# A two-layer spectral mixer on one core: batch 0's spectra made twice for one filter tile

## The chip, the cores and the metric

The kernel runs on one core of a Trainium2 chip. Its time is the device time of one launch in microseconds (us). The core has a matrix engine (TensorE, PE in the profile), three engines for elementwise work (VectorE or DVE, ScalarE or ACT, GpSimd or POOL) and a queue engine (SyncE or SP). Each takes its own instructions in order and waits for the others by semaphores. Data move by DMA, issued from the queues of SP, ACT and POOL.

## The reference

```python
def _attn_ref(x, filt_r, filt_i):            # x: (8, 3136, 256)
    X = np.fft.rfft(x, axis=1)
    F = (filt_r + 1j * filt_i)[None, :, :]   # (1569, 256)
    return np.fft.irfft(X * F, n=x.shape[1], axis=1)

def _moe_ref(x, U, V, w_ch1, w_ch2):         # x is the result above
    h = x.transpose(0, 2, 1) @ U @ V         # rank 32 along the sequence
    u = x + h.transpose(0, 2, 1)
    return u + np.maximum(u @ w_ch1, 0.0) @ w_ch2   # 256 -> 1024 -> 256
```

## The kernel before, in words

The transform of length 3136 = 64 x 49 is done in two steps by matrix products. Step one is a transform over 64 rows (table `w64`). Step two is, for each of 32 residues s, a product with the table `t2[s]` (98 x 128), whose 128 outputs are 64 real and 64 imaginary parts of one group of frequencies. The spectrum is multiplied by the filter, which lies in the tile `ft`, and goes back by the table `g12` (128 x 98 for each s). The residues go in pairs: m = 0 to 15 stands for s = 2m and 2m + 1. The tables and the filter come in four parts (`PARTS`) of 8 residues, so a new part begins at m = 0, 4, 8 and 12.

Batch 0 is a prologue of its own. All of it is in this order:

- `load_x`, `load_rest`, `load_table`, `load_filters` issue the loads from POOL's queue: batch 0 of x in three chunks, the tables and the filter part by part, then batch 1 of x, then U, V and the two channel weights.
- `first_f1` does step one in twelve units of four matmuls each, and the odd last row at its end. ACT and DVE empty PSUM into `at`, two instructions a unit, one on each. `keep_on(n)` puts n matmuls without use into the PE queue, and `keep_in` does so on another tile.
- `first_a(m)` turns a pair into place (four matmuls) and ACT copies it to `a`.
- `first_mid` is a pipeline over m: `forward` makes the spectrum px (two matmuls), `both_products` multiplies it on DVE by two filter sections at once into `uv` (1024 columns), `back` (eight matmuls with the two sections of `g12`) makes pi, and ACT copies pi into `et` with two instructions. px is made two pairs ahead, `a` three pairs ahead.
- Then `et` is transposed into `e2`, while `f1_units(1, True)`, drawn with `next(fill)`, does step one of batch 1. Its 13 units are drawn at set places.

In the old filter layout the section 0 of `ft` holds the real filter on both halves of the 128 partitions and section 1 holds the imaginary one, minus on the second half. The loads fill partitions 0 to 48 alone. `swap_real` and `swap_imag` on DVE make the second halves, a part at a time, before the first pair that needs the part. The second section of `g12` is the first with its halves exchanged: part 0 is loaded ready (`gs`), the others are made by `swap_table` on POOL.

After the prologue comes the stream: groups of rows run through `mm1` (256 to 1024), a ReLU, and `mm2` (1024 to 256). All the other work of the later batches is put by hand into slots between these products (`put(slot, generator)`); a group of eight slots takes some 9 us. Batch 1's middle (`both_products` again) starts in slot 8.8 at 1.2 slots a pair, batch 2 uses `product`, which multiplies in three instructions on DVE.

Of the kernel before, what the change touches and what calls it, by code (L numbers as in the profile page):

```python
# [13 lines left out]
SEQ = 3136  # L14
# [12 lines left out]
def _consts():  # L27
# [22 lines left out]
    for s in range(NS):  # L50
        for j in range(49):
# [15 lines left out]
            else:  # L67
# [3 lines left out]
                g[s, j, o:o + 49] = ei.real * (2 if f else 1)  # L71
                g[s, 64 + j, o:o + 49] = -ei.imag * 2

    t2[0, :, 64] = 0
    t2[0, 49:, 64] = (-1.0) ** r
    g[0, 64] = 0
    g[0, 64, 49:] = (-1.0) ** r
    g *= ESC / n
    gs = np.concatenate([g[:, 64:], g[:, :64]], 1)
# [5 lines left out]
            np.ascontiguousarray(g.reshape(4, 8, 128, 98).transpose(0, 2, 1, 3)).astype(f16),  # L85
            np.ascontiguousarray(gs[0:8].transpose(1, 0, 2)).astype(f16))
# [3 lines left out]
def kernel(  # L90
# [13 lines left out]
    w64_np, s2_np, idn_np, fold_np, wp_np, t2_np, g_np, gs_np = _consts()  # L104
# [7 lines left out]
    gs_d = nc.inline_tensor(gs_np, name="gsd")  # L112
# [8 lines left out]
    BUFS = {"x": 1, "f": 1, "m": 4, "o": 2}  # L121

    def bank(tag, name):
        return ps.tile([128, 512], F32, tag=tag, bufs=BUFS[tag], name=name)

# [21 lines left out]
    def load_x(b, c, parts=None):  # L147
# [3 lines left out]
        for lo, hi in parts or ((c0[c], c0[c + 1]),):  # L151
            for h in range(2):
                m = (hi - lo) // 4
                nc.gpsimd.dma_start(
                    t[64 * h:64 * h + 64, (lo - c0[c]) * DM:(lo - c0[c] + 4 * m) * DM]
                    .rearrange("p (m e) -> p m e", m=m),
                    bass.AP(tensor=x.tensor, offset=x.offset + (b * SEQ + 2 * lo + 4 * h) * DM,
                            ap=[[RD, NQ], [8 * DM, m], [1, 4 * DM]]))
            if hi == NH:
# [3 lines left out]
                nc.gpsimd.dma_start(t[0:64, o:o + DM], rows(x, b, NR - 1, 1))  # L163
# [9 lines left out]
    nyq = sb.tile([128, DM], F32, tag="ocho", bufs=1, name="nyq")  # L173
    PARTS = ((0, 8), (8, 16), (16, 24), (24, 32))
    for a, b in PARTS:
        for c in (0, NS * DM):
            nc.vector.memset(ft[32:64, c + a * DM:c + b * DM], 0.0)  # L177

    def load_table(k, a, b):

        dst, src, w = ((t2, t2_d, 128), (g12, g_d, 98))[k]
        n, p = (b - a) * w, dst.shape[0]
        nc.gpsimd.dma_start(dst[:, a * w:b * w],
                            bass.AP(tensor=src, offset=a // 8 * p * n, ap=[[n, p], [1, n]]))

    def swap_table(a, b):

        o = NS * 98
        for p, q in ((0, 64), (64, 0)):
            nc.gpsimd.tensor_copy(g12[p:p + 64, o + a * 98:o + b * 98],  # L190
                                  g12[q:q + 64, a * 98:b * 98])

    def load_filters(a, b):

        d = max(a, 1)
        for c, src in ((0, filt_r), (NS * DM, filt_i)):
            nc.gpsimd.dma_start(
                ft[0:24, c + a * DM:c + b * DM],
                bass.AP(tensor=src.tensor, offset=a * DM, ap=[[64 * DM, 24], [1, (b - a) * DM]]))
            nc.gpsimd.dma_start(  # L200
                ft[25:49, c + d * DM:c + b * DM].rearrange("p (k d) -> p k d", d=DM),
# [3 lines left out]
    def load_rest():  # L205

        for c, src in ((0, filt_r), (NS * DM, filt_i)):
            nc.gpsimd.dma_start(
                ft[25:49, c:c + DM],
                bass.AP(tensor=src.tensor, offset=32 * DM, ap=[[64 * DM, 24], [1, DM]]))  # L210
            nc.gpsimd.dma_start(
                ft[24:25, c:c + NS * DM],
                bass.AP(tensor=src.tensor, offset=24 * 64 * DM,
                        ap=[[NS * DM, 1], [1, NS * DM]]))
        nc.sync.dma_start(
            nyq[64:65, :],
            bass.AP(tensor=filt_r.tensor, offset=(SEQ // 2) * DM, ap=[[DM, 1], [1, DM]]))

    def swap_real(a, b):

        nc.vector.tensor_copy(ft[64:128, a * DM:b * DM], ft[0:64, a * DM:b * DM])

    def swap_imag(a, b):

        fb = NS * DM
        if a == 0:
            nc.vector.memset(ft[0:1, fb:fb + DM], 0.0)
        nc.vector.tensor_scalar_mul(ft[64:128, fb + a * DM:fb + b * DM],
                                    ft[0:64, fb + a * DM:fb + b * DM], -1.0)
# [3 lines left out]
    for c in range(1, len(CH)):  # L233
        load_x(0, c)
# [4 lines left out]
    for k, part in enumerate(PARTS):  # L239
        if k:  # L240
            load_table(0, *part)
        load_filters(*part)
        if k == 0:
            load_table(0, *part)
        load_table(1, *part)
        if k == 0:
            nc.gpsimd.dma_start(g12[:, NS * 98:(NS + 8) * 98], gs_d.ap())
        if k > 1:
            swap_table(*PARTS[k - 1])
    load_x(1, 0)  # L250
# [3 lines left out]
    load_x(1, 1)  # L254
    swap_table(*PARTS[3])
    load_x(1, 2)
    vqs = []
    for k in range(2):
        v = sb.tile([128, SEQ // 2], F16, tag="xt", bufs=5, name="vq")
        vqs.append(v)  # L260
        nc.gpsimd.dma_start(v[64:96, :], moe_V[:, k * (SEQ // 2):(k + 1) * (SEQ // 2)])
    w1 = cst.tile([128, 2 * 1024], F16)
    for i in range(4):
        nc.gpsimd.dma_start(
            w1[32 * i:32 * i + 32, :].rearrange("p (h c) -> p h c", h=2),
            bass.AP(tensor=moe_w_ch1.tensor, offset=moe_w_ch1.offset + i * 64 * 1024,
                    ap=[[1024, 32], [32 * 1024, 2], [1, 1024]]))
    w2 = cst.tile([128, 8 * DM], F16)
    w2n = sb.tile([128, 8 * DM], F16, tag="esb", bufs=2, name="w2n")
    nc.gpsimd.dma_start(w2n, moe_w_ch2.rearrange("(cc t) e -> cc (t e)", t=8))  # L270
# [6 lines left out]
    def v_order():  # L277

        for r in range(0, NR, 8):
# [8 lines left out]
            yield  # L288

# [60 lines left out]
    def keep_in(tile, n):  # L350

        for _ in range(n):
            nc.tensor.matmul(tile[:, 0:128], w64[:, :], idn[:, :],
                             start=True, stop=True, skip_group_check=True)

    def first_f1():
        ne = 0
# [582 lines left out]
```

## Time and profile before

| what | value |
|---|---|
| time, median of 3 runs | 525.0 us (524.52 to 525.54) |
| the profiled execution | 523.76 us, its span 522.0 us |
| busy share of the span | PE 95%, DVE 78%, ACT 72%, POOL 58% |
| DMA | 93.99 MB, mean 180 GB/s |
| granted TensorE clock | 1.000 |
| first product of batch 0 on DVE (L524) | starts at 19.98 us |
| last product of batch 0 ends | 44.16 us |
| first `mm1` of the stream (L712) | starts at 53.61 us |

The busy share is an average over stages that have different limits. PE leads over the whole, but the change is made in the first 54 us and in the DVE work of the slots that follow. There the timeline of each engine and the table by stages say more than the page. An idle time is put down to the instruction whose end released it. Lines such as L524 are lines of the kernel as printed above.

### The profile page before, as it was taken

The numbers are of one execution on the slowest core, as the hardware profiler recorded it, in microseconds if no ns is written. First come the engines' busy times: TensorE is split into PE (matmuls) and PEld (weight loads), VectorE is DVE, ScalarE is ACT, GpSimd is POOL, SyncE is SP. The second block draws the span as 40 slices with busy tenths as digits, with TensorE's granted clock in tenths as the row PEclk, the third lists the DMA queues.
The fourth block names the chain that finished last, engine by engine and source line by source line (L and its number), as shares of the span: only waits on it lengthen the run. The fifth ranks groups of instructions, "written<-read, shape, count | busy, mean of one in ns | idle before, by whom it ended". The sixth has DMA issues, their size and how long they took to land.

```text
span 522.0 us, 11372 instructions
## 1 busy us (share of the span) xinstructions
PE 496.7 (95%) x3976; PEld 327.4 (63%) x3976; DVE 407.7 (78%) x585; ACT 377.5 (72%) x772; POOL 301.9 (58%) x430
## 2 busy tenths in 40 slices
PE   4878899999989999999999999999999999999997
PEld 3766477777656665666666666666666666555555
DVE  7897386677888888998998888988999877436654
ACT  2767757768778768887788878888777678665552
POOL 7798733445765757775777675965666564313001
PEclk9999999999999999999999999999999999999999
DMA  8989998978899798887898698888777575644325
GB/s 135 188 143 221 233 214 203 213 209 191 197 202 253 180 203 181 215 219 176 235 216 221 162 253 207 184 227 194 180 194 150 129 167 134 139 100 80 71 62 121
DMA packets 122571, 93.99 MB, mean 180 GB/s; under 512 B 58017, under 2 KB 104866, under 8 KB 122514
## 3 DMA queue, kind: packets, MB, share of 16 engines
q1 hardware_dynamic: 98986, 50.93, 39.1%
q0 software_dynamic: 20240, 40.60, 37.9%
q10 hardware_dynamic: 3288, 1.74, 1.3%
q8 instruction: 31, 0.51, 0.4%
q14 instruction: 26, 0.21, 0.1%
HBM read 56.25 MB, written 48.17 MB: 200 GB/s over the span
## 4 chain that ended last, share of the span: by engine, by line
PE 78%; DVE 9%; DMA 6%; POOL 3%; issue 2%; ACT 1%; ACTq 0%; SPq 0%; DVEq 0%; POOLq 0%
PE phh L712 28%; PE po L789 25%; PE px L516 5%; PE pi L552 5%; PE pu L637 4%; PE po L738 4%; DVE uv L537 4%; DMA xt<-in_x_dram 3%; PE pf L472 3%; PE ph L594 2%; DVE ft L177 1%; DVE uv L535 1%; DMA out_dram<-och 1%; DMA g<-gd 1%; DMA a<-c 1%
## 5 line engine op out<-in xcount | busy, mean ns | idle before, releaser
L720 ACT ACTIVATE h<-phh 128x512 f16<-128x512 f32 (+1 forms) x391 | 205.4, 578 | 68.6 <-PE phh L712 64.1
L712 PE MATMUL phh<-ut,w 128*128 128x512 f16 x768 | 197.5, 379 | 0.3 <-ACT h L720 0.3
L540 POOL TENSOR_TENSOR y<-uv 128x512 f16<-128x512 f16 x96 | 111.8, 1165 | 100.1 <-DVE uv L537 80.3
L789 PE MATMUL po<-h,w 128*128 128x512 f16 x656 | 168.5, 379 | 0.0
L712 PEld LDWEIGHTS <-w 128*128 128x128 f16 x832 | 114.2, 144 | 54.5 <-issue 0.9
L537 DVE TENSOR_TENSOR uv<-px,ft 64x512 f16<-64x512 f32 x192 | 132.1, 688 | 2.6
L807 POOL DMA_DIRECT2D out_dram<-och x148 | 85.9, 588 | 81.6 <-DVE och L799 38.9
L789 PEld LDWEIGHTS <-w 128*128 128x128 f16 x656 | 60.5, 98 | 57.8 <-issue 1.1
L535 DVE TENSOR_TENSOR uv<-px,ft 128x512 f16<-128x512 f32 x96 | 64.9, 676 | 35.2 <-PE px L516 33.0
L556 ACT CAST esb<-pi 98x512 f16<-98x512 f32 x112 | 65.9, 589 | 32.1 <-PE pi L552 28.2
L798 DVE TENSOR_TENSOR tt<-po,ut 128x512 f32<-128x512 f32 x82 | 56.7, 692 | 34.3 <-PE po L789 32.3
L799 DVE STREAM_TRANSPOSE och<-tt 128x512 f32<-128x512 f32 x82 | 58.4, 712 | 2.8
L516 PE MATMUL px<-a,t 98*128 98x256 f16 x256 | 49.1, 273 | 5.6 <-DVE uv L537 2.8
L478 ACT CAST asb<-pf 128x512 f16<-128x512 f32 (+1 forms) x80 | 46.1, 576 | 6.5 <-PE pf L472 3.8
L524 DVE TENSOR_TENSOR uv<-px,ft 128x1024 f16<-128x1024 f32 x32 | 38.0, 1219 | 11.7 <-PE px L516 11.2
L702 ACT CAST ut<-pu 128x512 f16<-128x512 f32 x82 | 44.8, 612 | 0.0
L516 PEld LDWEIGHTS <-t 98*128 98x128 f16 x256 | 22.7, 98 | 31.6 <-DVE uv L537 10.6
L552 PE MATMUL pi<-y,g 128*98 128x256 f16 x192 | 36.7, 272 | 0.1
L472 PE MATMUL pf<-xt,w 128*128 128x512 f16 (+1 forms) x91 | 33.2, 370 | 1.0 <-DMA xt<-in_x_dram 1.0
L738 PE MATMUL po<-w,h 128*128 128x256 f16 x256 | 33.2, 273 | 0.0
L552 PEld LDWEIGHTS <-g 128*98 128x98 f16 x256 | 29.6, 123 | 3.2 <-issue 0.8
L637 PEld LDWEIGHTS <-e 96*128 96x128 f16 x686 | 26.4, 98 | 7.2
(99 smaller groups left out, 420.0 us busy)
## 6 DMA issues: line engine op xcount, KB each, us to landing
xt<-in_x_dram POOLq DMA_DIRECT2D x46, 256.0 KB, 6.6
out_dram<-och SPq DMA_DIRECT2D x180, 64.0 KB
a<-c SPq DMA_DIRECT2D x28, 384.0 KB
e<-c SPq DMA_DIRECT2D x56, 192.0 KB
out_dram<-och POOLq DMA_DIRECT2D x148, 64.0 KB, 3.5
c<-esb SPq DMA_DIRECT2D x24, 384.0 KB
c<-asb POOLq DMA_DIRECT2D x30, 256.0 KB, 5.6
out_dram<-och POOLq DMA_DIRECT2D x12, 256.0 KB, 4.8
```

Of the source, the lines that this page charges most:

```text
L516: nc.tensor.matmul(px[:, sl * DM:(sl + 1) * DM], t2[:, s * 128:(s + 1) * 128], a2[:, (2 * ml + sl) * DM:(2 * ml + sl + 1) * DM], start=Tru ...
L535: nc.vector.tensor_mul(uv[:, 0:512], px[:, :], ft[:, a:a + 512])
L537: nc.vector.tensor_mul(uv[p:p + 64, 512:1024], px[q:q + 64, :], ft[q:q + 64, b:b + 512])
L540: nc.gpsimd.tensor_add(y, uv[:, 0:512], uv[:, 512:1024])
L552: nc.tensor.matmul(pi[0:98, sl * DM:(sl + 1) * DM], g12[:, g:g + 98], y[:, o:o + DM], start=(fi == 0), stop=(fi == nf - 1), skip_group_che ...
L556: nc.scalar.copy(split(esb[:, ml * 512:(ml + 1) * 512]), natural(pi[0:98, :]))
L712: nc.tensor.matmul(pm[:, 0:w], w1[:, dh * 1024:(dh + 1) * 1024].rearrange("p (c t) -> p t c", t=8)[:, t], ut[:, dh * w:(dh + 1) * w], star ...
L720: nc.scalar.activation(h[:, 0:w], pm[:, 0:w], RELU)
L789: nc.tensor.matmul(po[:, :], w2[:, t * DM + dh * 128:t * DM + (dh + 1) * 128], hs[gx, t][:, :], start=(t == 0), stop=(t == 7))
L798: nc.vector.tensor_add(tt, po[:, :], uts[gx][:, dh * 512:(dh + 1) * 512])
L799: nc.vector.transpose(och.rearrange("p (j h a) -> p h j a", h=2, a=32)[:, dh], tt.rearrange("p (j t) -> p j t", t=32))
L807: (nc.gpsimd if k and (b < nb - 1 or r0 > 12) else nc.sync).dma_start(dst, och[32 * i:32 * i + 32, k * 512:(k + 1) * 512] .rearrange("p (r ...
```

## The change

1. **Spectra.** In the prologue `forward` gives way to eight matmuls of 64 weight columns each, which put the real spectrum on both halves of one PSUM bank and the imaginary one on both halves of the next. The tile px has two banks, two such tiles take the place of the four banks "m" while `first_mid` runs (`four_banks(k)` opens and closes the pools).
2. **Filter tile.** The real filter is loaded to partitions 0 to 49, the imaginary one to 64 to 113, in one section. Batch 0 needs no copy of it. The full two-section layout that batches 1 to 7 use is made later by `spread_filters` on DVE: twelve copies in slots 0 to 17, and four negations in slots 27 to 44.
3. **Tables.** The second section of `g12` is made for all four parts: the first half by a copy on DVE (`swap_table`), the second by a negation on ACT (`negate_table`). POOL does none of it, and `gs` is not loaded. POOL's queue has t2, filters and g of a part, with the next part's filters ahead of its t2.
4. **Order.** `first_a` stands ahead of the making of px in each turn. The odd row of batch 0 is loaded ahead of the last chunk, and `first_row` runs before the last four units. Each unit of `first_f1` is emptied by one engine (ACT for even, DVE for odd units). The `keep_on` counts are a list, and `keep_in` is gone. Of the 13 fills, one instead of four lies inside the loop, two follow it, five instead of four lie in the transposes.
5. **Weights.** V and w1 are issued after batch 1 of x as before, then batch 2's first chunk, then w2, then the POOL copies of V with batch 2's second chunk and the copies of w2 in the middle. The fills of batch 2 start at slot 5.2 instead of 4. Two output DMAs of batch 1 go from SP's queue to POOL's.

```diff
-    def swap_real(a, b):
-        nc.vector.tensor_copy(ft[64:128, a * DM:b * DM], ft[0:64, a * DM:b * DM])
-    def swap_imag(a, b):
...
-        nc.vector.tensor_scalar_mul(ft[64:128, fb + a * DM:fb + b * DM],
-                                    ft[0:64, fb + a * DM:fb + b * DM], -1.0)
+    def spread_filters():
+        for a, b in PARTS:
+            lo, hi = slice(a * DM, b * DM), slice((NS + a) * DM, (NS + b) * DM)
+            for dst, src in ((ft[0:64, hi], ft[64:128, lo]), (ft[64:128, hi], ft[64:128, lo]),
+                             (ft[64:128, lo], ft[0:64, lo])):
+                nc.vector.tensor_copy(dst, src)
+                yield
+        for a, b in PARTS:
+            neg = ft[64:128, (NS + a) * DM:(NS + b) * DM]
+            nc.vector.tensor_scalar_mul(neg, neg, -1.0)
+            yield
...
     def swap_table(a, b):
         o = NS * 98
-        for p, q in ((0, 64), (64, 0)):
-            nc.gpsimd.tensor_copy(g12[p:p + 64, o + a * 98:o + b * 98],
-                                  g12[q:q + 64, a * 98:b * 98])
+        nc.vector.tensor_copy(g12[0:64, o + a * 98:o + b * 98], g12[64:128, a * 98:b * 98])
+    def negate_table(a, b):
+        o = NS * 98
+        nc.scalar.mul(g12[64:128, o + a * 98:o + b * 98], g12[0:64, a * 98:b * 98], -1.0)
...
     def first_f1():
+        gaps = iter([18, 4, 8, 4, 40, 3, 3, 3, 22, 0, 0, 0])
         for r0 in range(0, NH - 1, 4):
+            if r0 == 16:
+                keep_on(next(gaps))
+                first_row(xs)
             for dh in range(2):
-                keep_on(4 if r0 < 16 else 0)
+                if r0 != 16 or dh:
+                    keep_on(next(gaps))
...
-        pxs = [ahead(0), ahead(1)]
-        keep_on(8)
-        for m in range(NS // 2):
...
+        def ahead(m):
+            px = pm[-1].tile([128, 1024], F32, tag="px", bufs=2, name="px")
+            for fi in range(2):
+                for sl in range(2):
+                    s, o = 2 * m + sl, fi * 512 + sl * DM
+                    for q in (0, 64):
+                        nc.tensor.matmul(
+                            px[q:q + 64, o:o + DM], t2[:, s * 128 + fi * 64:s * 128 + fi * 64 + 64],
+                            st[0]["a"][m // 4][:, s % KG * DM:(s % KG + 1) * DM],
+                            start=True, stop=True, tile_position=(0, q), skip_group_check=True)
+            return px
+        load_weights()
+        with four_banks(1):
+            keep_on(6)
+            pxs = [ahead(0)]
+            first_a(2)
+            pxs.append(ahead(1))
+            for m in range(NS // 2):
+                uv = sb.tile([128, 1024], F16, tag="uv", bufs=3, name="uv")
+                fap = ft[:, 2 * m * DM:2 * (m + 1) * DM]
+                nc.vector.tensor_mul(
+                    uv.rearrange("p (f e) -> p f e", f=2),
+                    pxs.pop(0).rearrange("p (f e) -> p f e", f=2),
+                    bass.AP(tensor=fap.tensor, offset=fap.offset, ap=[fap.ap[0], [0, 2], [1, 512]]))
+                if m % 4 == 0:
+                    swap_table(*PARTS[m // 4])
+                if pend is not None:
+                    back(*pend)
+                pend = (m, uv)
+                if m + 3 < NS // 2:
+                    first_a(m + 3)
+                if m % 4 == 0:
+                    negate_table(*PARTS[m // 4])
+                if m + 2 < NS // 2:
+                    pxs.append(ahead(m + 2))
+                if m == NS // 2 - 1:
+                    next(fill)
...
+    for t in (0, 1, 2, 3, 4, 5, 6, 7, 8, 11, 14, 17, 27, 30, 36, 44):
+        put(t, spread)
```

## The prediction

> **What bounds the kernel now.** I read the page first: over the whole span PE carries the chain that ended last.
>
> ```profile
> PE 78%; DVE 9%; DMA 6%; POOL 3%; issue 2%; ACT 1%; ACTq 0%; SPq 0%; DVEq 0%; POOLq 0%
> ```
>
> The 9% of DVE and 6% of DMA lie almost wholly in the first 65 us, which the change rewrites. From the first `mm1` on PE is full, so a microsecond by which the stream starts earlier is a microsecond of the result. The second view is the table by stages, cut at the marks of the prologue. Its columns are the length, then busy time of PE, PEld, DVE, ACT and POOL, the granted clock, DMA share and rate.
>
> ```profile
> 10.40:19.90 9.50, 6.48 (x64) 5.96 (x65) 6.90 (x16) 5.61 (x12) 6.33 (x10) 1.00 1.07 201
> 19.90:44.20 24.30, 20.39 (x313) 17.55 (x313) 23.77 (x22) 16.68 (x47) 21.39 (x33) 1.00 0.93 161
> 44.20:53.60 9.40, 8.44 (x108) 5.48 (x107) 6.33 (x13) 6.70 (x13) 8.37 (x13) 1.00 1.08 222
> 53.60:64.90 11.30, 9.71 (x53) 5.44 (x53) 2.98 (x6) 9.30 (x19) 8.01 (x15) 1.00 1.05 242
> 64.90:76.00 11.10, 10.54 (x80) 7.77 (x79) 8.84 (x10) 6.54 (x12) 4.52 (x9) 1.00 1.08 242
> ```
>
> From 19.9 to 44.2 DVE is busy 23.77 of 24.30 us. That loop is DVE's. What fills it stands in the timeline of DVE:
>
> ```profile
> 17.91 0.69 DVE L221 COPY ft<-ft 64x2048 f16<-64x2048 f16 x1
> ...
> 19.98 4.62 DVE L524 TENSOR_TENSOR uv<-px,ft 128x1024 f16<-128x1024 f32 x4
> 24.63 0.69 DVE L221 COPY ft<-ft 64x2048 f16<-64x2048 f16 x1
> 25.24 1.32 DVE L228 TENSOR_SCALAR ft<-ft 64x2048 f16<-64x2048 f16 x1
> 26.67 4.62 DVE L524 TENSOR_TENSOR uv<-px,ft 128x1024 f16<-128x1024 f32 x4
> ```
>
> Four products take 4.62 us, then two filter copies hold up the next part for 2.04 us. The last product ends at 44.16. For what PE would do in the new loop I used its timeline in one turn and at the end of the loop:
>
> ```profile
> 21.27 0.52 PE L413 MATMUL pi<-g,uv 128*128 128x98 f16 x8 [0.15 <-DVE uv L524]
> 21.62 0.39 PE L353 MATMUL px<-idn,w 128*128 128x128 f16 x4
> 21.85 0.38 PE L516 MATMUL px<-a,t 98*128 98x256 f16 x2
> 22.07 0.39 PE L394 MATMUL pt<-idn,at 128*98 128x128 f16 x4
> ```
> ```profile
> 43.78 0.38 PE L472 MATMUL pf<-xt,w 128*128 128x512 f16 x1
> 44.09 0.51 PE L323 MATMUL pu<-uq,w 64*64 64x512 f16 x4
> 44.44 0.18 PE L329 MATMUL pu<-uq,w 64*64 64x32 f16 x1
> ```
>
> The starts give PE's pace: back 0.35 us, px 0.22 for two, pt 0.22. The L323 row is the nearest to the new spectra: four matmuls of 64 weight columns with 512, 512, 256 and 256 columns, by halves of the partitions. One after the other they would take 0.64 us, at the 0.215 us that 512 columns take elsewhere (L472, 46.69 to 46.90); they took 0.35. So two such run beside each other. But L323 starts 0.31 us after a matmul of 512 columns, 0.09 more than that one needs: going over to the small form costs about 0.09 us, and again on the way back.
>
> **The change, part by part.** The sum is made against the profiled execution, 523.76 us (span 522.0 and 1.76 around it); the median of the three runs is 1.24 us above it.
>
> Start of the loop. All of `at` was ready at 17.98 (ACT) and the first product began at 19.98. After, the loads of x keep their order, and DVE's nine memsets still end at 10.39, so it can empty nothing before. I follow ACT, which now takes whole units: the second chunk is used at 12.0 as before; units at 12.4 and 13.3, the odd row at 15.1, two units at 15.8 and 16.65, each 0.43 per instruction, end near 17.5. Then pt 0.4, the copy 0.58, PE 0.7 and the first product at about 19.45: **-0.5**. Only two `first_a` precede it, and no filter copy is in its way. This supposes that the 40 `keep_on` matmuls after the fourth unit run at 0.056 us each. Bounds -1.5 to +2.9, the upper one in the rivals.
>
> The loop. Removed from DVE: three pairs of filter copies (2.0, 2.2 and 1.4 us). Added: four copies of 64x784, by L221's rate 0.69 x 784/2048 = 0.26, with its access 0.3 each. DVE's need is 16 x 1.155 + 4 x 0.3 = 19.7 instead of 24.2 us. PE's need per pair: back 0.35, pt 0.22, px as four pairs of 256 columns 0.43, two changes of form 0.18: 1.18 us beside DVE's 1.23. ACT's: 0.48 + 0.47 for its three copies (by their starts), and a negation per part: 64x784 lies between 98x512 at 0.58 and 128x1024 at 1.01, so 0.8, or 0.2 a pair: 1.15. The three are level, which leaves no room to catch up.
>
> And there is a new wait. `back(4k)` needs the negated table of its part. ACT makes it only after the copies of `back(4k-1)` and of `first_a(4k+3)`. I followed one turn by the starts above: PE could begin `back(4k)` 1.85 us after product 4k began, the negation is done after 2.9. For 1.1 us PE stands, and behind `back(4k)` stand pt and px, for which DVE waits. The px made ahead absorbs half of it the first time and less later. I take 0.6 each, 2.4 in all (bounds 0 and 4.4): the loop takes 22.1, **-2.1**. The table and filter loads are now issued without POOL's copies between (6 x 0.98 us) and without `gs`; I set their landing ahead of need, with the DMA share at 0.93 as the warning.
>
> Tail. Three fills move behind the loop. PE 3 x 0.22, on DVE 3 x 0.69; DVE has about 1.5 us idle while the last `back` goes through ACT. **+0.3** (0 to 1.0). `prep_u` now waits for the px banks; it did its work in the same place before, so nothing.
>
> First slots. POOL now waits for batch 1's first chunk to be used before it issues batch 2's, and w2 and the V copies stand behind that. The fourth fill comes about 2.6 us after the loop, near 44; V's first four steps take 4.9, w2's landing was 8.4 after issue, its copies 2.0: all by about 55.5. `mm2` reads it first at 63.0 before, about 60.5 after. So nothing there. PE waited 1.0 us for batch 2's x (at 57.7 and 62.8) and 0.3 for batch 1's readback. That x is now issued some 2.5 us earlier and used 1.2 slots later: **-0.8** (-1.3 to 0).
>
> Filter spreading. Twelve copies at 0.69 are 8.3 us of DVE, nine of them in slots 0 to 8. The stage 53.6 to 64.9 has 8.3 us of DVE free and takes 6.2; the next has 2.3 and takes 2.1. A copy holds what queues behind it (a ReLU, a PSUM copy whose bank PE wants) for up to 0.7. **+0.6** (0 to 2). The four negations, 0.69 to 1.32 each, and two output DMAs on POOL: nothing, at most 0.5.
>
> Sum: -0.5 - 2.1 + 0.3 - 0.8 + 0.6 = -2.5. 523.76 - 2.5 + 1.24 = **522.5 us**.
>
> [...]
>
> **The rivals.** No collision (0.25). If the negation is done in time, or px ahead covers it, the loop is 19.7: 2.4 less, 520.1. For it: ACT is busy only 16.68 of 24.30 us in this stage now. Against: its queue is in order and the negation stands last.
>
> PE takes the bound (0.12), the case on the other side. If pairs in the small form do not overlap with other weights between them, px takes eight times 0.108, 0.86, and a pair 0.86 + 0.57 + 0.18 = 1.61; PE's loop of 13 full pairs and three short ones, with part of the negation waits, comes to 27 us instead of 24.2. It decides from 1.23 us a pair on. 522.5 + (27 - 22.1) = 527.4. For: one row with other lengths is all that I have; against: that row, and L594, where 49 matmuls of 256 columns in quarters take 1.52 us. [...]
>
> A slow PE at the start (0.07). In the trace matmuls of 128 columns start 107 ns apart up to 16.7 us (four L366 in 0.43), and 56 ns apart from 18.1 on, though the clock column says 1.00. If the 40 and 22 extra ones run at 107, they take 6.6 instead of 3.5, and the first product comes near 22.3: 2.9 later than taken, 525.4. Against: PE was slow for the first 4.6 us of unbroken work from 12.0 on; after the change it works without a gap over 0.3 us from 3.3.
>
> The spreading costs (0.08). With POOL at work the copies may take 1.32 as L228 did: 15.8 us against 10.6 free in the two stages, 5.2 over, 4.6 more than taken: 527.
>
> The tables come late (0.08). If a part takes 5.8 us to land, each loop part waits some 0.3: 523.7. The change would then not do what its order says.
>
> **How the numbers follow.** The forecast has 0.40, the rivals 0.25, 0.12, 0.07, 0.08 and 0.08. A measurement of this kernel can tell about 0.2% from no change, 1.05 us. Faster: most of the forecast (0.37), no collision (0.25) and late tables (0.06): 0.68. Slower: PE's bound and the spreading (0.20) and a fifth of the forecast's unfavourable ends with the slow start (0.01): 0.21. The rest, 0.11, is the same. The range goes from 518.6 (no collision with an early start) to 526.5.
>
> **What would show it.** Right: no L221-like copy between the products; products of one part 1.15 to 1.2 apart, and a DVE wait for px of 0.5 to 1.1 us once in each part, with PE's wait for the negation; the last product near 41.6; the first `mm1` near 51; PE's waits for x gone. Wrong: product spacing near 1.6 (pairs do not overlap), 1.15 throughout (no collision), a first product after 21 (slow PE), waits of the products for DMA (tables), or an `mm1` that starts early while PE idles in the first 20 slots more than the 2.2 us of now.

## The result and the profile after

The changed kernel takes 527.72 us (median of 6 runs, 526.63 to 529.9), the kernel before 524.42 us beside it (522.93 to 525.54): the ratio is 1.0069, its 95% interval 1.0041 to 1.0098. The change makes the kernel slower by 3.3 us; 522.5 was forecast, and 526.5 was the upper end. The profiled execution has 526.80 us, with a span of 525.0 against 522.0.

The chain and the table by stages, for the changed kernel. The stages are cut at the first product of batch 0, its last product, the first `mm1`, the place where PE begins to wait for batch 1's readback (61.9) and the end of the low clock (72.0); the columns are those of the prediction's table.

```profile
PE 81%; DVE 7%; DMA 6%; POOL 2%; issue 2%; ACT 1%; DVEq 0%; POOLq 0%; SPq 0%
```
```profile
10.40:18.80 8.40, 6.88 (x105) 5.84 (x103) 5.10 (x13) 4.88 (x11) 5.86 (x11) 1.00 1.06 188
18.80:42.50 23.70, 19.42 (x299) 14.55 (x300) 20.75 (x21) 18.40 (x48) 15.00 (x27) 1.00 1.07 195
42.50:52.20 9.70, 9.13 (x111) 5.75 (x111) 8.07 (x16) 7.00 (x14) 6.93 (x11) 1.00 0.68 134
52.20:61.90 9.70, 8.79 (x48) 5.02 (x46) 9.47 (x12) 8.51 (x19) 7.45 (x9) 1.00 0.82 206
61.90:72.00 10.10, 6.17 (x27) 3.73 (x26) 4.50 (x6) 1.78 (x3) 6.96 (x13) 0.66 0.98 206
```

PE has gained and DVE lost share in the chain, as the edit means, and the loop's DVE has fallen from 23.77 to 20.75 us of work. But in the last line PE works 6.17 of 10.10 us at a granted clock of 0.66; in the kernel before, it worked 10.54 of 11.10 us at 1.00 in the nearest stage (64.9 to 76.0). DVE's timeline in the new loop:

```profile
18.89 1.22 DVE L450 TENSOR_TENSOR uv<-px,ft 128x1024 f16<-128x1024 f32 x1 [1.82 <-DMA ft<-in_filt_i_dram]
20.15 0.39 DVE L194 COPY g<-g 64x784 f16<-64x784 f16 x1
20.57 4.80 DVE L450 TENSOR_TENSOR uv<-px,ft 128x1024 f16<-128x1024 f32 x4
25.40 0.36 DVE L194 COPY g<-g 64x784 f16<-64x784 f16 x1
25.79 2.36 DVE L450 TENSOR_TENSOR uv<-px,ft 128x1024 f16<-128x1024 f32 x2
29.08 2.46 DVE L450 TENSOR_TENSOR uv<-px,ft 128x1024 f16<-128x1024 f32 x2 [0.94 <-PE px L435]
```

The filter copies are gone, a short copy of the table stands once in each part, and px is late once in each part but the first. PE's timeline shows why: seven of the eight matmuls of `back` wait for ACT's negation, 0.67 us in the first part and 1.07 in each of the others.

```profile
20.73 0.22 PE L420 MATMUL pi<-g,uv 128*128 128x98 f16 x1
21.62 0.46 PE L420 MATMUL pi<-g,uv 128*128 128x98 f16 x7 [0.67 <-ACT g L199]
21.92 0.39 PE L402 MATMUL pt<-idn,at 128*98 128x128 f16 x4
22.24 0.63 PE L435 MATMUL px<-a,t 98*64 98x256 f16 x8
22.80 0.52 PE L420 MATMUL pi<-g,uv 128*128 128x98 f16 x8
```

| mark, us of the span | before | after | shift | forecast of the shift |
|---|---|---|---|---|
| first product of batch 0 | 19.98 | 18.89 | -1.1 | -0.5 |
| last product ends | 44.16 | 42.43 | -1.7 | -2.6 |
| first `mm1` | 53.61 | 52.27 | -1.3 | -2.3 |
| first spectrum (px) of batch 1 | 64.45 | 65.92 | +1.5 | about -2.5 |
| end of the span | 522.0 | 525.0 | +3.0 | -2.5 |

So the prologue gained, and everything was lost between the first `mm1` and 72 us. Three views of the changed kernel show how: POOL's timeline, SP's, and PE's.

```profile
45.22 1.18 POOL L157 DMA_DIRECT2D xt<-in_x_dram  x2 [5.29 <-PE pf L500]
46.37 0.59 POOL L294 DMA_DIRECT2D w2n<-in_moe_w_ch_dram  x1
47.00 5.41 POOL L275 COPY low<-vq 32x256 f16<-32x256 f16 x8
52.36 1.62 POOL L157 DMA_DIRECT2D xt<-in_x_dram  x2
```
```profile
49.05 5.22 SPq L511 DMA_DIRECT2D c<-asb  x6
54.37 0.58 SPq L514 DMA_DIRECT2D c<-asb  x1
61.89 2.82 SPq L524 DMA_DIRECT2D a<-c  x6
```
```profile
65.92 0.59 PE L543 MATMUL px<-a,t 98*128 98x256 f16 x2 [3.93 <-DMA a<-c]
66.30 0.63 PE L500 MATMUL pf<-xt,w 128*128 128x512 f16 x1
66.72 1.91 PE L739 MATMUL phh<-ut,w 128*128 128x512 f16 x4
```

POOL stands 5.29 us until batch 1's first chunk of x is used. Nothing else is queued for the DMA engines meanwhile. The columns here are those of the stages; the first line is of the kernel before, the next two of the kernel after:

```profile
42.00:44.00 2.00, 1.94 (x31) 1.44 (x30) 2.00 (x2) 1.95 (x6) 0.76 (x2) 1.00 1.11 193
```
```profile
43.00:45.00 2.00, 1.79 (x24) 1.19 (x25) 1.90 (x6) 1.07 (x4) 0.00 (x0) 1.00 0.08 16
45.00:47.00 2.00, 2.00 (x33) 1.76 (x31) 1.90 (x4) 1.73 (x3) 1.74 (x3) 1.00 0.45 17
```

The loads that should have filled these 4 us run later, beside SP's writes of batch 1's first transform (`c<-asb`). The last write, issued at 54.37, landed at 61.67; the readback `a<-c`, which needs it, could be issued only at 61.89 and landed at 65.88. Before, the last write was issued later (55.70) and the readback earlier (59.70). SP's and PE's timelines of the kernel before:

```profile
55.70 0.55 SPq L486 DMA_DIRECT2D c<-asb  x1
59.70 11.04 SPq L496 DMA_DIRECT2D a<-c  x8
```
```profile
64.45 0.39 PE L516 MATMUL px<-a,t 98*128 98x256 f16 x2 [0.29 <-DMA a<-c]
```

I call the time from the issue of the last write to the readback's arrival the round trip: 55.70 to 64.40, 8.7 us, before; 54.37 to 65.88, 11.5, after. It has two parts: from the issue of the last write to the issue of the readback (the write part, 4.0 us before and 7.5 after), and from there to the arrival (the read part, 4.7 before and 4.0 after). So the change lengthened the write part. In it the DMA engines are not busy throughout, as a row of the kernel after shows:

```profile
60.00:62.00 2.00, 1.98 (x14) 1.39 (x13) 1.99 (x2) 1.12 (x3) 2.00 (x3) 1.00 0.05 13
```

PE idles until the readback arrives, and then its clock is low:

```profile
64.00:66.00 2.00, 0.08 (x1) 0.13 (x2) 0.00 (x0) 0.00 (x0) 1.96 (x5) 0.77 1.17 258
66.00:68.00 2.00, 2.00 (x6) 0.85 (x6) 1.46 (x2) 0.18 (x1) 0.05 (x1) 0.50 1.14 205
68.00:70.00 2.00, 2.00 (x9) 1.14 (x8) 1.26 (x2) 1.49 (x3) 1.06 (x2) 0.50 1.17 203
70.00:72.00 2.00, 2.00 (x13) 1.62 (x12) 0.45 (x2) 0.11 (x1) 1.78 (x4) 0.52 1.10 280
72.00:74.00 2.00, 2.00 (x16) 1.55 (x15) 1.97 (x3) 1.09 (x2) 0.00 (x0) 1.00 1.06 229
```

Four matmuls of `mm1` take 1.91 us here (L739 above) where 1.03 is usual.

### The profile page after: what moved, and what is told of

Same layout as the page of the kernel before. It is cut to its first block, busy times and chain, and to the rows that moved or that the text cites. A ratio compares the mean times of both kernels' runs of the same rounds, so it can differ in the third digit from the quotient of the medians.

```text
span 525.0 us, 11534 instructions
## 1 busy us (share of the span) xinstructions
PE 501.8 (96%) x4055; PEld 328.6 (63%) x4055; DVE 418.7 (80%) x598; ACT 378.9 (72%) x773; POOL 300.8 (57%) x425
## 4 chain that ended last, share of the span: by engine, by line
PE 81%; DVE 7%; DMA 6%; POOL 2%; issue 2%; ACT 1%; DVEq 0%; POOLq 0%; SPq 0%
PE phh L739 29%; PE po L816 26%; PE px L543 5%; PE pi L579 5%; PE po L765 4%; DVE uv L564 4%; PE pu L664 4%; PE pf L500 3%; DMA xt<-in_x_dram 3%; PE ph L621 2%; DVE uv L562 2%; DMA c<-asb 1%; DMA g<-gd 1%; DMA a<-c 1%; PE pu L679 1%
## 5 line engine op out<-in xcount | busy, mean ns | idle before, releaser
L739 PE MATMUL phh<-ut,w 128*128 128x512 f16 x768 | 198.4, 380 | 0.8 <-DVE asb L504 0.7
L739 PEld LDWEIGHTS <-w 128*128 128x128 f16 x832 | 114.3, 144 | 56.0 <-issue 2.5
L834 POOL DMA_DIRECT2D out_dram<-och x150 | 87.8, 592 | 78.1 <-DVE och L826 42.1
L543 PE MATMUL px<-a,t 98*128 98x256 f16 x224 | 43.8, 277 | 7.8 <-DMA a<-c 3.9
L506 ACT CAST asb<-pf 128x512 f16<-128x512 f32 (+1 forms) x77 | 44.3, 577 | 5.8 <-PE pf L500 4.4
L543 PEld LDWEIGHTS <-t 98*128 98x128 f16 x224 | 20.1, 99 | 33.2 <-DVE uv L564 11.7
L157 POOL DMA_DIRECT2D xt<-in_x_dram x50 | 30.4, 615 | 8.8 <-PE pf L500 5.3
```

The lines of the kernel that those rows point to most:

```text
L543: nc.tensor.matmul(px[:, sl * DM:(sl + 1) * DM], t2[:, s * 128:(s + 1) * 128], a2[:, (2 * ml + sl) * DM:(2 * ml + sl + 1) * DM], start=Tru ...
L739: nc.tensor.matmul(pm[:, 0:w], w1[:, dh * 1024:(dh + 1) * 1024].rearrange("p (c t) -> p t c", t=8)[:, t], ut[:, dh * w:(dh + 1) * w], star ...
L834: (nc.gpsimd if k and (b < nb - 1 or r0 > 12) or b == 1 and n == 0 and r0 < 8 else nc.sync).dma_start(dst, och[32 * i:32 * i + 32, k * 512 ...
```

## The experiments

My theory after this comparison: batch 2's loads, held by POOL's stand, collide with batch 1's round trip through memory, and the half clock that follows doubles the harm. Rivals: the filter spreading in DVE's queue, and the negation in the loop.

**Moving the loads.** Two orders of POOL's queue, and the reverse test on the kernel before. Lines of the second list are in the order of issue.

```diff
 a1   if k == 3:
-         load_x(2, 1)
          (copies of w2)
+         load_x(2, 1)
 a2   order: w2n, three steps of V, load_x(2, 0), V, w2, load_x(2, 1)
 b1 (kernel before)   load_x(2, 1) behind four steps of V, not behind all
```

> The kernel after, with batch 2's second chunk of x issued behind the two copies of w2 instead of ahead of them (about 58.7 instead of 52.4 us). Collision theory (that load competes with the last writes of batch 1's step one, whose readback PE then awaits for 3.9 us, after which its clock stands at half for some 6 us): writes land about 4 us earlier, PE's wait for the readback under 1 us, clock 1.00, perhaps 1 to 2 us of wait for the moved x itself; about 523 us, 4 to 5 below the kernel after. Spreading theory (the twelve filter copies in VectorE's queue make the last writes late): nothing changes, about 527.5 us.

527.38 us, ratio 1.0050 (1.0024 to 1.0076). The second chunk was issued at 59.00, 1.0 ahead of the readback (60.02), and PE waited 4.1 for that. The collision moved from the writes to the readback: the write part is 5.3 us long instead of 7.5, the read part 6.4 instead of 4.0, and the round trip stayed about as long (11.7 against 11.5).

> The kernel after, with w2 issued ahead of batch 2's first chunk, that chunk after two steps of the V copies, and the second chunk behind all V copies and w2 copies. POOL's 5.3 us stand for the first chunk's buffer should then cost no DMA time, since w2 lands in the stretch 43 to 47 us in which the DMA engines are idle now. Collision theory: readback lands before it is needed or nearly so, clock 1.00, x never awaited for more than 0.5 us; 521 to 522 us, the prologue's 1.3 us and more below the kernel before. Spreading theory: 527 us.

528.03 us, 1.0070 (1.0044 to 1.0097), a miss; the wait is 3.4 in the profiled execution, which with 525.33 us was one of the fastest. POOL's stand was still there (first chunk at 45.49), and the second chunk and the third then came together.

> The kernel before, with one edit: batch 2's second chunk of x issued after three steps of the V copies, near 52.4 us instead of 56.0. [...] Spreading theory (no filter copies are in this kernel's slots): no change, 524.4 us.

525.65 us, 1.0019 (0.9996 to 1.0041), the wait for the readback 2.0 instead of 0.3. By the collision theory I had expected a wait of 2 to 4 us and 527 to 531 us. The direction is that of the theory; the size is inside the interval, and the time lies below that range.

**The price of the half clock.**

```diff
+    put(8.8, one(keep_on, 70))
```

> The kernel after, with 70 matmuls without use put ahead of the first spectrum of batch 1, in the 4 us that PE waits for the readback; the loads are as they were. If the wait and the half clock are two costs (collision theory, with a clock that falls in an idle stretch), the readback still lands near 65.9 us, the clock stays 1.00, and 2.5 to 3 us come back: about 525 us. If the low clock has another cause (power, or the load of the engines), it stays low at 66 to 72 us and the time is 527 to 528 us.

525.79 us, 1.0022 (1.0003 to 1.0041). The clock is 1.00 throughout. A first part of the readback had landed at 65.33, and the first px starts at 65.89, behind the 70 matmuls, which end at 65.84; so it starts where it did in the changed kernel (65.92). The 1.9 us by which the median lies under 527.72 go to the clock, net of a new wait of 1.4 us for ACT's copy (`esb`).

**Taking the second load out.** Batch 2 reads its first chunk twice; the load of the second is left out.

```diff
-                load_x(2, 1)
+                st[2]["x"][1] = st[2]["x"][0]
```

> The kernel after, with batch 2's second chunk of x left out: its units read the first chunk instead, so batch 2's result is not the reference's. It takes out the one load that is issued at 52.4 us. Collision theory: batch 1's writes end before 59 us, the readback lands near 62 us, PE's wait for it is under 0.5 us, clock 1.00, 521 to 522 us. If that load is not what delays them: the wait stays at 3 us or more and the time near 526 us.

523.63 us, 0.9992 (0.9972 to 1.0013), clock 0.999. SP's and PE's timelines:

```profile
55.73 0.61 SPq L514 DMA_DIRECT2D c<-asb  x1
60.11 10.62 SPq L524 DMA_DIRECT2D a<-c  x8
```
```profile
64.04 0.38 PE L543 MATMUL px<-a,t 98*128 98x256 f16 x2 [0.94 <-DMA a<-c]
```

The wait is 0.9 and the round trip 8.3, with a write part of 4.4 us instead of 7.5. One load of 512 KB is worth 4.1 us by the medians, more than the whole loss (the profiled execution, 525.30 us, lies 1.7 above its median). All the spreading copies are still in this kernel, so the rival that puts the loss down to them is out. The run settles that this load is the cause; whether by its place or by its bytes, the orders of the queue below have to show. The pause of the DMA engines is in both kernels (share 0.05 from 60 to 62 us after, 0.01 from 59 to 61 us in d3), each time from some 2 us ahead of the readback's issue on. What differs lies ahead of the pause: from the issue of the last write the engines stay busy some 5.3 us in the changed kernel, some 2.5 in d3.

**The loop.** The negation one turn earlier (e1), the first four fills in the last turns of the loop so that POOL's stand ends earlier (c1), and both (f1).

```diff
 e1
+                if m == 0:
+                    negate_table(*PARTS[0])
                 if m + 3 < NS // 2:
                     first_a(m + 3)
-                if m % 4 == 0:
-                    negate_table(*PARTS[m // 4])
+                if m % 4 == 3 and m < 12:
+                    negate_table(*PARTS[m // 4 + 1])
 c1   (also: the two fills behind the loop go, four instead of five lie in the transposes)
-                if m == NS // 2 - 1:
+                if m >= 12:
                     next(fill)
```

> The kernel after, with each part's negation on ScalarE one turn ahead of the part (part 0's ahead of the copy of a). Negation theory of the prediction: PE's four waits for the negated table (3.9 us in all) go, the last product ends near 39.5 instead of 42.4 and the first mm1 starts near 49.5 instead of 52.3. For the whole: if writes, loads and readback all hang on the fills, everything moves by 2.9 us and the time is near 525; if the amount of DMA work sets the readback, it stays near 65 us and nothing is gained, 527 to 528 us.

525.12 us, 1.0019 (1.0001 to 1.0038). The negation waits are gone, the last product ends at 40.05 and the first `mm1` starts at 49.90, 2.4 earlier than after. The whole gain of the loop reaches the end, 2.6 us below the changed kernel; but the readback moved by 2.7 with all the rest, and PE still waited 3.60 us for it.

> The kernel after, with the first four fills (batch 1's step one) drawn in the last four turns of the loop and four in the transposes, as before the change. Backlog theory (POOL waits 5.3 us for the buffer of batch 1's first chunk, the DMA engines stand idle from 43 to 47 us, and 2 MB of x and w2 then run in the very stretch in which batch 1's writes and readback must pass): POOL's stand is under 2 us, batch 2's first chunk and w2 are in by 48 us, PE's wait for the readback is under 1 us, clock 1.00; 521 to 522.5 us. If the writes and the readback are late for another reason (their own size, the order in SP's queue): the wait of some 4 us stays, 526 to 528 us.

533.34 us, 1.0173 (1.0136 to 1.0210). A miss. What the four fills did in the loop is read from f1, which has the same fills.

> Both edits together: the first four fills inside the loop and the negations a turn ahead. Backlog theory with the negation theory: no wait for the readback over 1 us, clock 1.00, first mm1 near 49.5: 518.5 to 520 us, under both kernels. If the amount of DMA work is the bound: readback awaited for 3 us and more, clock low, 525 us or more.

530.23 us, 1.0121 (1.0095 to 1.0148): a miss too. VectorE empties these fills; the copy waits in its queue for PE, 1.18 and 1.67 us between the last products, and the next product stands behind it. PE in turn waits 1.69 for a product, and its clock is then at 0.50 from 40.1 to 50.3 (the table by stages of f1):

```profile
42.00:44.00 2.00, 1.16 (x12) 0.60 (x10) 2.00 (x4) 0.55 (x2) 0.00 (x0) 0.50 0.91 169
```

The first `mm1` starts at 56.69, and POOL still stands 4.21. How much of the loss is the wait and how much the half clock was not taken apart. Neither run tests what it was for.

**Taking POOL's stand away.** Batch 2's first chunk gets a buffer of the output tiles, free at that time (h1); the same with e1's edit (h2). In g1 the fills lie in the loop and ScalarE empties them, with e1's edit.

```diff
 h1   w1's loads
+        st[2]["x"] = {0: sb.tile([128, 8 * DM], F16, tag="och", bufs=2, name="xt")}
         load_x(2, 0)
 g1 (with c1 and e1)
-                if both and (ne % 2 if b > 1 else ne not in (3, 5, 7, 9, 12)):
+                if both and (ne % 2 if b > 1 else ne > 3 and ne not in (5, 7, 9, 12)):
```

> The kernel after, with batch 2's first chunk of x loaded into a buffer of the output tiles (free until the first output), so that POOL need not wait for the buffer of batch 1's first chunk. Backlog theory: POOL's stand of 5.3 us goes; that chunk and w2 are issued near 41 us and land in the stretch 43 to 47 us that is idle now; the second chunk is issued near 47 and in by 52; batch 1's last writes (from 54.4) meet no load, the readback lands near 61.5, PE waits for it under 0.7 us, clock 1.00: 521 to 522.5 us. If the readback is late by the size of the writes and of itself: wait 3 us or more, 526 us or more.

525.64 us, 1.0010 (0.9987 to 1.0033), above the forecast. The first chunk is issued at 41.65, the wait for the readback is gone and the clock is 1.00. Waits of 1.5 (a PSUM bank behind VectorE's ReLU) and 1.4 (`esb`) stand in its place.

> The same, with the negations a turn ahead (which took 2.5 us off in the kernel after). Backlog theory: first mm1 near 49.9, readback awaited under 1 us, clock 1.00: 518.5 to 520.5 us, faster than the kernel before by 0.8 to 1%. If the DMA work up to the readback is the bound: the wait is 2.5 us or more and the time 522 to 524 us.

522.82 us, 0.9962 (0.9939 to 0.9984): faster than both kernels, though less so than I expected. The first `mm1` starts at 49.83, and PE doesn't wait for the readback. PE's timeline, then DVE's:

```profile
56.09 0.44 PE L503 MATMUL pf<-xt,w 128*128 128x512 f16 x1 [1.60 <-DVE h L748]
```
```profile
50.73 4.71 DVE L230 COPY ft<-ft 64x2048 f16<-64x2048 f16 x4
55.36 0.68 DVE L748 TENSOR_SCALAR h<-phh 128x512 f16<-128x512 f32 x1
```

The ReLU of the second `mm1` stands behind four spreading copies, 4.71 us long, and a fill behind the ReLU's bank.

> The kernel after with the negations a turn ahead and the first four fills inside the loop, emptied by ScalarE as before the change (in the earlier try VectorE emptied them, and each product then queued behind a copy that waited for PE). If that queueing was what cost the earlier try 5 us: products stay 1.2 us apart, no wait of VectorE for the fills, the first mm1 near 50, POOL's stand under 1.5 us, and with the backlog gone 519 to 521 us. If the fills in the loop cost by themselves (PE and x landing late): 526 us or more.

522.68 us, 0.9968 (0.9948 to 0.9988), again less than expected. ScalarE's emptying of the fills does not hold up the products: PE waits 0.3 us for one, where it waited 3.3 in all in f1. POOL stands only 1.01, the first `mm1` starts at 51.05; PE waits 2.4 for the readback and 1.9 for the ReLU.

**The spreading.** h2 with POOL's copies of w2 behind all of V's (k1), with the twelve copies spread to slots 0 to 22 (k2), and with none at all (k3: the four negations are left out as well, and the products of batches 1 to 7 read the one section in place of both, so that their filters are others).

```diff
 k1           (copies of w2 behind the loop over v_order, not at k == 3)
 k2
-    for t in (0, 1, 2, 3, 4, 5, 6, 7, 8, 11, 14, 17, 27, 30, 36, 44):
+    for t in (0, 3, 6, 8, 10, 12, 14, 16, 17, 19, 21, 22, 27, 30, 36, 44):
         put(t, spread)
 k3   (both lines away; the products read one section twice)
```

> As h2_own_buffer_negate (522.8 us), but GpSimd makes all copies of V before any of w2. If GpSimd's copies beside the spreading copies are what makes them 1.1 to 1.3 us long instead of 0.69, the order changes little where V is copied meanwhile and the first four stay near 1.2; if w2's copies are what doubles them, they fall to 0.7 and the ReLU wait of 1.6 falls under 0.8, 521.5 to 522.3 us. If the spreading is not what holds the ReLU, 522.8.

526.19 us, 1.0028 (1.0004 to 1.0051). The first four copies take 3.84 us instead of 4.71 (the median of all twelve is 0.69 instead of 0.87), and the ReLU wait falls from 1.6 to 0.7: so far as expected. But the wait for the readback is back, 3.4 us.

> As h2_own_buffer_negate, but the twelve spreading copies stand in slots 0, 3, 6, 8, 10, 12, 14, 16, 17, 19, 21, 22 instead of 0 to 8, 11, 14, 17. If the four copies in a row hold the ReLU, PE's wait of 1.6 for it goes and the time is 521.2 to 522.0. If VectorE is simply full in these slots, the waits come back later in slots 9 to 22, and the time stays within 0.5 of 522.8.

526.60 us, 1.0039 (1.0010 to 1.0068). No ReLU wait; wait for the readback 3.0.

> As h2_own_buffer_negate, without the twelve spreading copies and the four negations: the products of batches 1 to 7 read the single-section filter, so their filters are not the reference's; the number and shape of the products is unchanged. If the spreading costs what the prediction took (0.6), 522.2 us; if it costs the 1.6 of the ReLU wait and more, 520.5 to 521.2; if the loss is elsewhere, 522.8.

525.50 us, 1.0009 (0.9984 to 1.0034). With the suspected cost taken away altogether the kernel is slower than h2, with 4.9 us of wait. All three expectations fail. POOL's, SP's and PE's timelines of this run:

```profile
56.20 1.18 POOL L157 DMA_DIRECT2D xt<-in_x_dram  x2
```
```profile
57.63 14.57 SPq L527 DMA_DIRECT2D a<-c  x8
```
```profile
63.86 0.58 PE L546 MATMUL px<-a,t 98*128 98x256 f16 x2 [4.91 <-DMA a<-c]
```

Without VectorE's copies beside them POOL's copies of w2 and the last six of V take 2.01 and 3.13 us here, where they took 2.74 and 4.86 in h2. So POOL issues batch 2's *third* chunk at 56.20 (k1, by its other order: 55.48), ahead of the readback; in h2 it came at 58.63, 1.3 us behind it.

**Moving the third load.** k3, k1 and k2 with idle memsets in POOL's queue ahead of the third chunk (l1, l2, l3), and h2 with that load ahead of the last of V's copies (l4).

```diff
 l1, l2, l3 (10, 12, 5 times)
+                        nc.gpsimd.memset(pad, 0.0)
                         load_x(2, 2)
 l4
+            if k == 4:
+                load_x(2, 2)
```

> As k3_no_spread (525.5 us, 4.9 us of PE's wait for batch 1's readback), with ten memsets in GpSimd's queue ahead of the load of batch 2's third chunk, so that it is issued some 3.5 us later, near 59.7, behind the readback (57.6) instead of ahead of it (56.2). If that load is what holds the readback, the wait falls under 1, the clock stays at 1.00 and the time comes to 519 to 521.5 us; what h2_own_buffer_negate (522.8) has above it is then the price of the spreading. If something else holds the readback, the wait and the 525.5 stay.

523.22 us, 0.9978 (0.9954 to 1.0003): 2.3 us below k3.

> As k1_w2_last (526.2 us, wait 3.4), with twelve memsets ahead of the third chunk's load: issued near 59.7 instead of 55.5, the readback at 57.6. By the theory of the third chunk the wait falls under 1 and the time comes to 521 to 522.8 us; by the others it stays at 526.2.

522.74 us, 0.9980 (0.9952 to 1.0009): 3.5 below k1. Wait 1.3.

> As k2_spread_thin (526.6 us, wait 3.0), with five memsets ahead of the third chunk's load: issued near 60.8 instead of 59.0, the readback at 58.2. By the theory of the third chunk 1.8 us are enough, the wait falls under 1 and the time comes to 521 to 523.5 us; by the others it stays at 526.6.

523.75 us, 0.9999 (0.9977 to 1.0020): 2.9 below k2. But k2's own profiled execution (524.03 us) was far below its median, and its round trip is no longer than that of l3, so for this pair only the medians speak.

> As h2_own_buffer_negate (522.8 us, no wait for the readback), with the third chunk's load ahead of the last of V's copies: issued near 56 instead of 58.6, ahead of the readback (57.3) instead of behind it. By the theory of the third chunk the readback's wait comes back at 2.5 to 5 us, the clock falls to 0.5 for some microseconds, and the time goes to 525 to 527.5 us; by the others nothing changes, 522.8.

526.87 us, 1.0042 (1.0015 to 1.0070): 4.1 above h2. POOL's, SP's and PE's timelines of l4:

```profile
49.24 1.19 POOL L157 DMA_DIRECT2D xt<-in_x_dram  x2
58.35 1.43 POOL L157 DMA_DIRECT2D xt<-in_x_dram  x2
```
```profile
52.00 0.56 SPq L519 DMA_DIRECT2D c<-asb  x1
59.28 4.93 SPq L529 DMA_DIRECT2D a<-c  x6
```
```profile
65.53 0.59 PE L548 MATMUL px<-a,t 98*128 98x256 f16 x2 [5.62 <-DMA a<-c]
```

Against the transfers of batch 1 two loads of x stand otherwise here than in h2. The second chunk is issued 2.8 us ahead of the last write, where it was 4.2; the edit doesn't touch it, but in this execution it came 1.5 later. The write part is 7.3 us instead of 5.4. So the readback is issued at 59.28 instead of 57.33, and the third chunk, only 0.3 us earlier by the clock than in h2, is 0.9 ahead of the readback instead of 1.3 behind it. The read part is 6.2 instead of 4.4 at most. Some 2 us lie in each part; how the 4.1 of the medians is shared between the two loads, one profile can't tell.

The round trips and their parts from the profiles, one execution each. Where PE did not wait for the readback, its arrival is known only as not later than the first px, and the table says "to" that number. c1 is left out: its profiled execution took 590.7 us, far from its median.

| kernel | a load of x against the last write | a load of x against the readback | write part, us | read part, us | round trip, us |
|---|---|---|---|---|---|
| d3 | none near | none near | 4.4 | 3.9 | 8.3 |
| before | second chunk 0.3 behind | the same, 3.7 ahead | 4.0 | 4.7 | 8.7 |
| h1 | second 6.0 ahead | third 1.4 behind | 4.7 | to 4.0 | to 8.7 |
| b1, l2 | second 3.9 ahead | third 1.6, 5.6 behind | 5.6, 5.4 | 3.7, 4.0 | 9.4, 9.4 |
| h2, l1 | second 4.2, 5.1 ahead | third 1.3, 1.5 behind | 5.4, 5.5 | to 4.4, 4.1 | to 9.8, 9.6 |
| k2, l3 | second 3.2, 3.1 ahead | third 0.8, 2.4 behind | 6.2, 6.1 | 3.7, 4.0 | 9.9, 10.1 |
| a2 | second and third 1.1 ahead | none near | 6.0 | 4.3 | 10.3 |
| e1, a3, after | second 2.4, 2.2, 2.0 ahead | third 1.9, 1.9, 1.6 behind | 6.9, 7.0, 7.5 | 3.9, to 4.3, 4.0 | 10.8, to 11.3, 11.5 |
| f1 | second 6.3 ahead | third 1.1 ahead | 4.4 | 6.3 | 10.7 |
| k1, g1, k3 | second 4.7, 4.8, 3.9 ahead | third 2.1, 0.4, 1.4 ahead | 5.6, 5.7, 5.7 | 5.5, 5.7, 6.2 | 11.2, 11.3, 11.9 |
| a1 | none near | second 1.0 ahead | 5.3 | 6.4 | 11.7 |
| l4 | second 2.8 ahead | third 0.9 ahead | 7.3 | 6.2 | 13.5 |

The two parts follow two loads. With a load of x issued in the 2.1 us ahead of the readback the read part is 5.5 to 6.4, without 3.7 to 4.7. With the second chunk 2.0 to 2.8 us ahead of the last write the write part is 6.9 to 7.5, at 3.1 and 3.2 it is 6.1 and 6.2, and in the other runs with one chunk it is 4.0 to 5.7; a2, with two chunks 1.1 ahead, has 6.0.

l1 to l3 don't bring the wait under 1 as I expected (2.7, 1.3, 3.1): PE now reaches the place at 59.4 to 61.6, earlier than any round trip ends.

## Why the prediction was wrong

**First slots, the step that failed.** The prediction put them at -0.8 and said of POOL's stand: "So nothing there." I asked when V, w2 and the third chunk would be needed, and all were in time. I did not ask beside what the transfers would run. The measured loss of this stage is in the marks: -1.3 at the first `mm1`, +1.5 at the first px of batch 1, so 2.8 us against the stream, and 1.5 more by the end of the span, where the half clock goes on. Of the terms, the gain of 1.0 for the waits for x came true (they are gone), and it was outweighed by the readback's wait (3.9 instead of 0.3) and the clock (1.9, from a3). d3 shows that the load of the second chunk is the cause (without it 523.63, and a readback wait of 0.9), h1 and h2 that POOL's stand makes it collide, and the two parts of the round trip how: beside it the writes took 7.5 us to the readback's issue instead of 4.0. The prediction's 0.3 for batch 1's readback was read from the trace of before as a small wait that would go; it was the end of a chain that was already on the path.

**The start**: -0.5 was forecast, -1.1 measured, and the slow PE (rival, 0.07) did not come. `at` was ready at 16.82 and not near 17.5; the 40 `keep_on` matmuls took 0.06 each, as supposed. The 1.82 beside the first product is DVE's idle time before it, and the filter's DMA is named there as the last release; but the px that the product reads ended only at 18.80, and the product began at 18.89. DVE follows a px by 0.04 elsewhere, so the filter cost 0.05 at most.

**The loop**: -2.1 forecast, -0.6 measured (24.18 to 23.54), with the mechanism as told. The sizes, from DVE's timeline: 16 products 19.24 us instead of 18.5; four copies 1.47 instead of 1.2 (0.36 to 0.39 each; the 0.04 that the prediction put on for the access was an estimate); the waits for px 0.94, 0.93 and 0.71, together 2.58 against 2.4; and 0.25 of short gaps. The products are longer for two reasons: one that stands alone or behind a copy or a wait takes 1.22 instead of 1.155, and in a row of four they take 4.80 instead of 4.62, since PE's turn by the starts is 1.24 (pt 0.32, px 0.56, back 0.36) and not 1.18. e1 shows what "no collision" would have given: 2.4 us at the end of the loop, as that rival had it. The pairs overlap: px takes 0.56, changes of form included, where the rival in which PE takes the bound had 0.86 and 0.18.

**The tail**: +0.3 forecast, 9.45 to 9.84 measured, +0.4.

**The spreading**: +0.6. The copies are 0.7 alone (the first line), 1.14 and 1.41 beside POOL's copies of w2 (the second), and 1.05 to 1.12 beside its copies of V (DVE's timeline of the changed kernel):

```profile
53.17 2.82 DVE L230 COPY ft<-ft 64x2048 f16<-64x2048 f16 x4
56.62 2.58 DVE L230 COPY ft<-ft 64x2048 f16<-64x2048 f16 x2
```

In the changed kernel this showed only as a 0.7 wait. The rival that gave it 4.6 more is out: d3 (523.63), l2 (522.74) and h2 (522.82) have all of it. Its own price stays open. Leaving it out altogether (l1, 523.22) gave nothing over keeping it (l2, h2), but in l1 PE waited 2.7 for the readback, and its profiled execution began the stream 2.7 us later than k3's (52.55 against 49.88), behind a half clock from 14.2 to 17.6 us.

**The range.** By the prediction's own terms its lower end would be 519.1 (520.1, and 1.0 for the earlier start) and not 518.6. Its upper end, 526.5, lies below two of its own rivals, 527.4 and 527, which had 0.20 of the chances. The measured time is near these two, but by neither of their mechanisms: the products are 1.2 us apart and not 1.6, and d3 keeps the spreading.

**What stays open.** h2 starts its stream 3.8 us earlier than before and ends 1.9 us earlier. At the first px of batch 1 it is still 2.7 ahead (61.72 against 64.45): PE did not wait for the readback there, but had waited 1.60 for the ReLU and run 3.4 us at half clock. Where the other 0.8 went, between there and the end, was not followed. How many of k2's executions collide can't be told from one profile.

## What to carry to other kernels

Of a step that delays a DMA issue, ask not only whether its data are in time, but what the engines do in the gap and which transfers it will run beside afterwards: a write and its readback through memory are a chain, and a load issued in the 2 us ahead of the readback, or in the 3 us ahead of the last write, cost 2 to 4 us here (d3, l1, l2 and l3 against their pairs, l4 against h2). A gain earlier in a kernel can move such an order by itself; so can a suspected cost that is taken away (k3). When the same wait comes back after each repair, list the issue times of all transfers near it, run by run, before forming the next theory.

## What the runs showed of the hardware

PE's clock after a pause is not a matter of the pause's length alone. In h2 it fell to 0.50 after an idle of 1.60 us, in l3 it stayed at 1.00 after one of 3.15 (the table by stages of h2, then of l3):

```profile
56.00:57.00 1.00, 0.91 (x3) 0.43 (x3) 0.97 (x2) 0.39 (x1) 1.00 (x3) 0.63 0.07 23
57.00:58.00 1.00, 1.00 (x3) 0.34 (x2) 0.96 (x2) 0.82 (x3) 1.00 (x2) 0.50 0.00 0
```
```profile
63.00:64.00 1.00, 1.00 (x5) 0.52 (x4) 1.00 (x1) 0.39 (x1) 0.55 (x1) 1.00 1.18 239
```

By the shares of the slices the stretches of half clock are 3.4 us long in h2 (56.3 to 59.7) and l1 (65.4 to 68.8), 6.8 after the change (65.1 to 71.9) and 10.2 in f1 (40.1 to 50.3). The idle at or just ahead of their start was 1.60 us in h2, 2.67 in l1, 3.93 after the change and 1.69 in f1 (there with further waits of up to 0.84 inside the stretch), so their length doesn't follow that of the pause alone. What else counts, no run here shows.
